# Late rows of an attention and feed-forward kernel: stores and loads moved to GpSimd's queue, differences to GpSimd, splits spread over steps, the order of the late part written out by hand

## The chip, the cores and the metric

One Trainium2 chip, one core. The metric is device time in microseconds (us) of one execution. Engines: PE (TensorE, matmuls), DVE (VectorE), ACT (ScalarE), POOL (GpSimd) and SP (SyncE, which here only issues transfers, "DMAs").

## The reference, cut to what matters

```
scores = q k^T / 8  + bias(distance, head);  only the last 96 keys and the first 8 are kept
a      = softmax(scores);   attn = a v          # 4 batches, 8 heads, 768 rows, 64 per head
x      = attn as 3072 rows of 512
out    = leaky_relu(x @ w_in, 0.01) @ w_out     # 512 -> 2048 -> 512, float32
```

## The kernel before

**Precision.** PE multiplies in a short float32 form, so every operand is kept as a high and a low part: `h = cast(x)` on ACT, then `l = x - h` on DVE ("a split"). Each product is three matmuls: high by high, low by high, high by low. Weights are `wih`, `wil` (first layer) and `woh`, `wol` (second).

**Feed-forward.** The 3072 rows are 24 attention steps of 128 rows. The first 18 are six plain chunks of three (384 rows, chunks 0 to 5). A chunk takes 16 *steps*; step `j` of 96 makes a block of 128 hidden values for a chunk (`hidden`, 12 matmuls L1031 to L1033 into `ps_h`), then PE does the output of the block before (`project`, 9 matmuls L1052 to L1054 into `ps_o`). Between the two stands a chain on other engines: ACT copies `ps_h` to `t` (L1035), DVE applies the leaky relu (L1036), ACT casts `gh` (L1041), DVE subtracts `gl` (L1042). `ps_h` is one buffer, so the next hidden block waits for the copy `t`; the output matmuls wait for `gh` and `gl`.

**The last six attention steps** (768 rows) go by Strassen's scheme, in eight *rounds* after step 95. A round has seven products of six matmuls (L611, into two banks `ps_p`), and in between 12 output groups of three matmuls for the round before (the first round has only three, those of step 95). Its inputs are the rows `b11`, `b12`, `b21`, `b22`, four differences of them (`t1` to `t4`, tile `diff`, L520), and sums of weight blocks `s1` to `s4`, which POOL makes ten additions a round (L541). Everything is split: rows at L516 (ACT) and L517 (DVE), sums at L547 and L548. In a round DVE also adds products (`u2`, `u3`, `t`, L629) and makes the four hidden blocks (`halves`, L622 to L624); ACT copies `u1` (L678) from the first product's bank before the third product may go on in it.

**Attention inside the steps.** In the late part attention is done in *visits* (two units each) put ahead of certain steps, `VISITS`. A visit's results for attention steps 15 to 23 can't stay on the chip: ACT copies them to `xo` (L355) and a DMA stores them to a buffer `xd` in memory (L356). Rows of chunk 5 are loaded back by `reload(j - RELOAD)` as one DMA into `xl` (L555) and split in four quarters, one in each of the next four steps (L558, L559). The rows of the Strassen part come back in `prepare(n)`, n = j - 96, at n = -4 (L512), and are split there and after.

**What sets the order.** Instructions under `pin` keep the program's order on their engine; the others are placed by a scheduler. PE's are all pinned. `pinned[0]` is set for each step: true up to step 22, for steps with a visit and while parts of a visit are left over; in the last steps and the Strassen part it is false, so there the scheduler chose. Waits are in order: an engine that waits for one instruction's input does nothing else. All DMAs of the main path but one are issued by SP.

Of the kernel before, what the change touches and what calls it, by code (L numbers as in the profile page):

```python
# [10 lines left out]
F32 = mybir.dt.float32  # L11
F32R = mybir.dt.float32r
# [6 lines left out]
P = 128  # L19
# [3 lines left out]
PAIRS = 22  # L23
HT = 384
SUPER = 2 * HT // P
VISITS = [39, 42, 46, 50, 54, 57, 61, 65, 68, 72, 76, 79, 83, 87, 90]
RELOAD = 70
TB = 32
G = 32
WIN = 96  # L30
# [21 lines left out]
def fast_path(ctx, tc, qp, kp, vp, wi, wo, nvec, weights, nmall, out, B, H, S):  # L52
# [45 lines left out]
    def pin(ins):  # L98

        if pinned[0]:  # L100
            tc.keep_in_program_order(ins)
# [248 lines left out]
    def high_x(u, av):  # L350
        if where(u)[0] >= SPILL:
            s, uu, i = where(u)
            units.pop(u)
            xo = att.tile([P, 2, P], F32, tag="work", name="xo", bufs=2)
            pin(nc.scalar.copy(out=xo, in_=av[:, :, 2 * KW:]))  # L355
            pin(nc.sync.dma_start(out=xd[:, 2 * uu:2 * uu + 2, (s - SPILL) * P:(s - SPILL + 1) * P], in_=xo))  # L356
            return
        pin(nc.scalar.copy(out=parts(u, 0), in_=av[:, :, 2 * KW:]))

# [145 lines left out]
        return n.rearrange("p (k t) -> p k t", k=2)  # L505

    def value(k):
        return late[k] if k in ("diff",) else late[k][1].bitcast(F32)

    def load_x(k):  # L510
        rows, cols = slice(2 * (k[1] == "2"), 2 * (k[1] == "2") + 2), slice(HT * int(k[2]), HT * int(k[2]) + HT)
        pin(nc.sync.dma_start(out=value(k), in_=xd[:, rows, cols]))  # L512

    def split_x(k, v=None):
        v = value(k) if v is None else v
        pin(nc.scalar.copy(out=late[k][0], in_=v))  # L516
        pin(nc.vector.tensor_tensor(out=late[k][1], in0=v, in1=late[k][0].bitcast(F32), op=ALU.subtract))  # L517

    def diff(in0, in1):
        pin(nc.vector.tensor_tensor(out=late["diff"], in0=value(in0), in1=value(in1), op=ALU.subtract))  # L520

    def block(n, f, m):
        return [weights[x][:, 2 * m:2 * m + 2, f * P:(f + 1) * P] for x in range(2)]
# [20 lines left out]
    def split_sum(i, k):  # L544
        if i >= NF // 2:
            return
        pin(nc.scalar.copy(out=late[k][0], in_=here[k]))  # L547
        pin(nc.vector.tensor_tensor(out=late[k][1], in0=here[k], in1=late[k][0].bitcast(F32), op=ALU.subtract))  # L548

    def reload(n):  # L550

        c = NCHUNK - 1
        if n == 0:
            xt[c] = [xts.tile([P, NK, CT], F32R, tag="xt", name=name) for name in ("xh", "xl")]
            pin(nc.sync.dma_start(out=xt[c][1].bitcast(F32), in_=xd[:, :, :CT]))  # L555
        elif 0 < n <= NK:
            hi, lo = (x[:, n - 1] for x in xt[c])
            pin(nc.scalar.copy(out=hi, in_=lo.bitcast(F32)))  # L558
            pin(nc.vector.tensor_tensor(out=lo, in0=lo.bitcast(F32), in1=hi.bitcast(F32), op=ALU.subtract))  # L559

# [2 lines left out]

    def prepare(n):

        if n == -4:
            early.close()
            pools["mem"] = mem = phase.enter_context(tc.tile_pool(name="late", bufs=1, side="right", reuse_waits="tile"))
            pools["ps"] = phase.enter_context(tc.tile_pool(name="ps_q", bufs=1, space=bass.MemoryType.PSUM, side="right", reuse_waits="tile"))
            pinned[0] = True  # L570
            for k in ("b11", "b21"):
                t = xts.tile([P, 4, HT], F32R, tag="xt", name=k)
                late[k] = [t[:, :2], t[:, 2:]]
            for k in ("b22", "t1", "t2", "t3", "t4"):
                late[k] = [mem.tile([P, 2, HT], F32R, name=k + x) for x in "hl"]
            late["b12"] = late["t3"]
            late["diff"] = mem.tile([P, 2, HT], F32, name="diff")
            for k in ("s1", "s2", "s3", "s4"):
                late[k] = [mem.tile([P, 2, P], F32R, name=k + x) for x in "hl"]
                here[k] = mem.tile([P, 2, P], F32, name=k)  # L580
            for k in ("b11", "b12", "b22", "b21"):
                load_x(k)
            make_sums(0)
        elif n == -3:
            diff("b12", "b11")
            split_x("t1", late["diff"])
            split_x("b11")
        elif n == -2:
            diff("b22", "diff")
            split_x("t2", late["diff"])  # L590
            diff("diff", "b21")
            split_sum(0, "s2")
            split_sum(0, "s3")
        elif n == -1:
            split_x("t4", late["diff"])
            diff("b22", "b12")
            split_x("t3", late["diff"])
            split_sum(0, "s1")

    def strassen():  # L600

# [23 lines left out]
            return gh, gl  # L625

        def add(name, in0, ps, op=ALU.add):
            t = mem.tile([P, HT], F32, name=name) if name else ffn.tile([P, HT], F32, name="t")
            pin(nc.vector.tensor_tensor(out=t, in0=in0, in1=ps, op=op))  # L629
            return t  # L630

# [26 lines left out]
        for i in range(NF // 2 + 1):  # L658
            if i:
                todo = [lambda n=n, g=g: second(g, n) for n in range(12)]  # L660
            else:
                todo = [lambda: ffn2(len(order) - 1, [n]) for n in range(3)]
                todo = [(lambda n=n: ffn2(len(order) - 1, [n])) for n in range(3)]

            def behind_(n):
                for _ in range(n):
                    if todo:
                        todo.pop(0)()
            if i == NF // 2:
                behind_(12)  # L670
                break
            b = blocks_of(i)
            x, y = banks[::-1] if i % 2 else banks
            gs = {}
            ps = x()
            product(b["a11"], "b11", ps)
            u1 = mem.tile([P, HT], F32, name="u1")
            pin(nc.scalar.copy(out=u1, in_=ps))  # L678
            split_sum(i, "s4")
            make_sums(i + 1)  # L680
            behind_(2 if i else 0)
            ps2 = y()
            product(late["s2"], "t2", ps2)
            u2 = add("u2", u1, ps2)
            split_sum(i + 1, "s2")
            if i == 0:
                split_x("b21")
            behind_(2 if i else 1)
            product(b["a12"], "b21", ps, first=False)
            t = ffn.tile([P, HT], F32, name="t")  # L690
            pin(nc.scalar.copy(out=t, in_=ps))
            gs[0, 0] = halves(t)
            behind_(2 if i else 1)
            product(late["s3"], "t3", ps2, first=False)
            u3 = add("u3", u1, ps2)
            split_sum(i + 1, "s3")
            if i == 0:
                split_x("b22")
            behind_(2 if i else 1)
            ps = x()  # L700
            product(late["s1"], "t1", ps)
            gs[1, 1] = halves(add(None, u3, ps))
            split_sum(i + 1, "s1")
            behind_(2)
            ps2 = y()
            product(b["a22"], "t4", ps2)
            gs[1, 0] = halves(add(None, u3, ps2, ALU.subtract))
            behind_(1)
            product(late["s4"], "b22", ps, first=False)
            gs[0, 1] = halves(add(None, u2, ps))  # L710
            behind_(12)
            g = i, gs
            if i == NF // 2 - 2:
                band_holds(tc, fl, nvec, nmall)
            if i == NF // 2 - 1:
                band_holds_everywhere(tc, fl, x()[0:1, 0:1], flag)
        phase.close()
        return flags[0]

# [23 lines left out]
    ps_o = ctx.enter_context(tc.tile_pool(name="ps_o", bufs=3, space=bass.MemoryType.PSUM))  # L743
    behind = []
    for j in range(len(order)):
        pinned[0] = j < half + NF or bool(behind) or any(t >= PAIRS for t in ev_at.get(j, ()))
        conv = list(conv_at.get(j, ()))
        for t in ev_at.get(j, ()):
            if t >= PAIRS:
                visit(t, behind)  # L750
            else:
                event(t, conv[:1])
            conv = conv[1:]

        def end():
            for step in due:
                step()
            due.clear()
            if behind:
                behind.pop(0)()  # L760

        def more():
            if behind:
                behind.pop(0)()
            for n, p in enumerate(conv):
                if n:
                    end()
                for step in conversion(p):
                    step()
        if j == half:  # L770

            scale_bias(tc, tabs[:, 1], nbw, H, 2)
            scale_bias(tc, tabs[:, 0, HALF:], nb0, H, 2)
        ffn1(j, end, more)
        if j:
            ffn2(j - 1)
        reload(j - RELOAD)
        prepare(j - len(order))
# [352 lines left out]
```

## Time and profile before

| what | value |
|---|---|
| three runs | 661.36, 663.00, 663.35 us; median 663.0 |
| the profiled execution | 661.57 us, of which the span of the profile is 660.0 |
| mean granted clock of PE | 0.986 |
| busy share | PE 95%, DVE 65%, ACT 44%, POOL 14% |

Times inside the profile count from the span's start. A step without a visit takes 4.2 us. Steps 70 and 71 lie at 372 to 395 us, the last visit (step 90) at 490, the first Strassen round at 524, the last output at 655. A line of the timeline gives start, duration, engine, line, operation, what is written and read, and in brackets how long the engine was idle before and what released it. "SPq" is the queue of DMAs that SP issues.

### The profile page before, as it was taken

To read this page: it belongs to the slowest core of one execution; us is meant where nothing else is said; L and a number is where in the kernel's file an instruction comes from. 1 tells how busy PE (TensorE), PEld (TensorE's weight loads), DVE (VectorE), ACT (ScalarE), POOL (GpSimd) and SP (SyncE) were. 2 spreads that over 40 slices of the span, in tenths; PEclk is the share of its full clock that TensorE was granted. 3 is DMA by queue.
4 is the path that set the end of the run, shared out by engine and by line. 5 is a ranking of instruction groups with operands and counts; after the bars stand their busy time and mean duration, and the time that the engine had idled before them with its cause. 6 is when DMAs were issued, how large, how long until landed. Compare 5 with 4: busy or idle time off the path is not lost. (4 is left out here: it accounts for less than half of the span.)

```text
span 660.0 us, 14710 instructions
## 1 busy us (share of the span) xinstructions
PE 629.0 (95%) x5692; PEld 550.8 (83%) x5692; DVE 429.1 (65%) x1191; ACT 293.0 (44%) x822; POOL 95.4 (14%) x128
## 2 busy tenths in 40 slices
PE   6699999999999999999999969999998899999996
PEld 4578898898888888988888858888886789888884
DVE  6888998886665475665755545565528676666642
ACT  6887755455443353444444424444325332222211
POOL 3213300000000000000000000000018255555300
PEclk9799999999999999999999979999999999999999
DMA  8876744414666345375656555557412010000002
GB/s 278 308 288 211 224 148 132 155 33 169 209 205 206 109 127 165 113 242 171 213 166 210 177 160 176 192 167 251 144 29 92 1 49 0 1 1 0 1 1 100
DMA packets 61677, 92.79 MB, mean 141 GB/s; under 512 B 10144, under 2 KB 36768, under 8 KB 61600
## 3 DMA queue, kind: packets, MB, share of 16 engines
q1 hardware_dynamic: 61456, 91.51, 42.9%
q8 instruction: 47, 0.77, 0.5%
q14 instruction: 30, 0.25, 0.1%
q10 hardware_dynamic: 144, 0.26, 0.1%
HBM read 70.26 MB, written 21.50 MB: 139 GB/s over the span
## 5 line engine op out<-in xcount | busy, mean ns | idle before, releaser
L1031 PE MATMUL ps_h<-xh,wih 128*128 128x384 f32 x384 | 133.7, 348 | 6.8 <-ACT t L1035 6.7
L1054 PE MATMUL ps_o<-woh,gl 128*128 128x512 f32 x336 | 133.9, 399 | 3.9 <-DVE gl L1042 3.7
L1052 PE MATMUL ps_o<-woh,gh 128*128 128x512 f32 x336 | 133.1, 396 | 0.6 <-ACT gh L1041 0.4
L1053 PE MATMUL ps_o<-wol,gh 128*128 128x512 f32 x336 | 132.6, 395 | 0.0
L1033 PE MATMUL ps_h<-xh,wil 128*128 128x384 f32 x384 | 130.2, 339 | 0.0
L1032 PE MATMUL ps_h<-xl,wih 128*128 128x384 f32 x384 | 130.1, 339 | 0.0
L1036 DVE SCALAR_TENSOR_TENSOR t<-t 128x384 f32<-128x384 f32 x96 | 57.7, 602 | 65.4 <-ACT t L1035 63.8
L1035 ACT COPY t<-ps_h 128x384 f32<-128x384 f32 x96 | 45.8, 477 | 122.1 <-PE ps_h L1033 121.9
L1031 PEld LDWEIGHTS ps_h<-xh,wih 128*128 128x128 f32 x384 | 72.6, 189 | 16.6 <-ACT t L1035 7.6
L222 ACT ACTIVATE pr<-pr,nmall 128x192 f32<-128x192 f32 (+1 forms) x192 | 83.6, 440 | 4.9 <-DVE nmall L207 4.9
L1054 PEld LDWEIGHTS ps_o<-woh,gl 128*128 128x128 f32 x336 | 63.2, 188 | 21.0 <-DVE gl L1042 6.5
L541 POOL TENSOR_TENSOR s<-wih 128x256 f32<-128x256 f32 x16 | 14.7, 922 | 455.4 <-PE ps_v L338 411.0
L1042 DVE TENSOR_TENSOR gl<-t,gh 128x384 fp32r<-128x384 f32 x96 | 54.4, 566 | 32.9 <-ACT gh L1041 32.9
L1032 PEld LDWEIGHTS ps_h<-xl,wih 128*128 128x128 f32 x384 | 72.7, 189 | 2.9
L1052 PEld LDWEIGHTS ps_o<-woh,gh 128*128 128x128 f32 x336 | 63.4, 189 | 11.5 <-ACT gh L1041 2.1
L1033 PEld LDWEIGHTS ps_h<-xh,wil 128*128 128x128 f32 x384 | 72.6, 189 | 0.1
L1053 PEld LDWEIGHTS ps_o<-wol,gh 128*128 128x128 f32 x336 | 63.2, 188 | 10.0
L1041 ACT CAST gh<-t 128x384 fp32r<-128x384 f32 x96 | 49.1, 511 | 44.6 <-DVE t L1036 43.9
L541 POOL TENSOR_TENSOR s<-s,wil 128x256 f32<-128x256 f32 x48 | 44.9, 940 | 3.0
L207 DVE CUSTOM_DVE_ANT_0 pr<-ps_v,nbw 128x192 f32<-128x192 f32 x88 | 25.3, 354 | 25.8 <-ACT xo L355 14.1
L623 ACT CAST gh<-t 128x384 fp32r<-128x384 f32 x32 | 16.4, 513 | 47.3 <-DVE t L622 45.6
L222 ACT ACTIVATION_READ_ACCUMULATOR pr<-pr,nmall 128x1 f32 x192 | 36.7, 191 | 0.0
(176 smaller groups left out, 926.0 us busy)
## 6 DMA issues: line engine op xcount, KB each, us to landing
kr<-in_kp_dram SPq DMA_DIRECT2D x40, 384.0 KB, 4.5
vr<-in_vp_dram SPq DMA_DIRECT2D x40, 320.0 KB, 5.1
via<-pr SPq DMA_DIRECT2D x30, 384.0 KB, 2.6
pt<-via SPq DMA_DIRECT2D x120, 96.0 KB, 2.4
wst<-in_wi_dram SPq DMA_DIRECT2D x16, 512.0 KB, 3.8
wst<-in_wo_dram SPq DMA_DIRECT2D x16, 512.0 KB, 4.1
qs<-in_qp_dram SPq DMA_DIRECT2D x24, 256.0 KB, 4.2
out_dram<-part SPq DMA_DIRECT2D x20, 256.0 KB, 2.9
```

The source lines that it names most:

```text
L222: pin(nc.scalar.activation(out=p, in_=p, func=AF.Exp, scale=-1.0, bias=nm[:, 2 * a + j:2 * a + j + 1], accum_out=sm[:, 2 * a + j:2 * a + j ...
L541: pin(nc.gpsimd.tensor_tensor(out=here[k], in0=acc_, in1=t, op=op))
L1031: tc.keep_in_program_order(nc.tensor.matmul(ps, lhsT=wih[:, k, fs], rhs=xh[:, k, :CT], start=(k == 0), stop=False))
L1032: tc.keep_in_program_order(nc.tensor.matmul(ps, lhsT=wih[:, k, fs], rhs=xl[:, k, :CT], start=False, stop=False))
L1033: tc.keep_in_program_order(nc.tensor.matmul(ps, lhsT=wil[:, k, fs], rhs=xh[:, k, :CT], start=False, stop=(k == NK - 1)))
L1035: pin(copy(out=t, in_=ps))
L1036: pin(nc.vector.scalar_tensor_tensor(out=t, in0=t, scalar=0.01, in1=t, op0=ALU.mult, op1=ALU.max))
L1041: pin(copy(out=gh, in_=t))
L1042: pin(nc.vector.tensor_tensor(out=gl, in0=t, in1=gh.bitcast(F32), op=ALU.subtract))
L1052: tc.keep_in_program_order(nc.tensor.matmul(o, lhsT=gh[:, ts_], rhs=woh[:, f, :], start=first, stop=False))
L1053: tc.keep_in_program_order(nc.tensor.matmul(o, lhsT=gh[:, ts_], rhs=wol[:, f, :], start=False, stop=False))
L1054: tc.keep_in_program_order(nc.tensor.matmul(o, lhsT=gl[:, ts_], rhs=woh[:, f, :], start=False, stop=last))
```

## The change

- Stores of `xo` and the loads of `xl` and of the `b` rows are issued by POOL instead of SP.
- `VISITS` moves up by up to two steps (last visit at 88, before 90); `RELOAD` is 68 instead of 70, and the four quarter splits of `xl` begin four steps after the load instead of one.
- The Strassen part's preparation is stretched from four steps to twelve: `b11`, `b21` are loaded at n = -12, `b12`, `b22` and the first sums at n = -8, one or two splits a step from n = -6. The four differences move from DVE to POOL and get two buffers.
- The check of the band (`band_holds`) moves from the last rounds to steps 88 and 89.
- From step 39 on everything goes in program order. In the rounds the code is put in another order: the additions that free a bank come before the leaky relu of the block ahead.

```diff
-VISITS = [39, 42, 46, 50, 54, 57, 61, 65, 68, 72, 76, 79, 83, 87, 90]
-RELOAD = 70
+VISITS = [39, 42, 46, 49, 53, 56, 60, 63, 67, 70, 74, 77, 81, 84, 88]
+RELOAD = 68
...
-            pin(nc.sync.dma_start(out=xd[:, 2 * uu:2 * uu + 2, (s - SPILL) * P:(s - SPILL + 1) * P], in_=xo))
+            pin(nc.gpsimd.dma_start(out=xd[:, 2 * uu:2 * uu + 2, (s - SPILL) * P:(s - SPILL + 1) * P], in_=xo))
...
-        pin(nc.sync.dma_start(out=value(k), in_=xd[:, rows, cols]))
+        pin(nc.gpsimd.dma_start(out=value(k), in_=xd[:, rows, cols]))
...
-    def diff(in0, in1):
-        pin(nc.vector.tensor_tensor(out=late["diff"], in0=value(in0), in1=value(in1), op=ALU.subtract))
+    def diff(name, in0, in1):
+        t = pools["mem"].tile([P, 2, HT], F32, tag="diff", name="diff", bufs=2)
+        pin(nc.gpsimd.tensor_tensor(out=t, in0=value(in0), in1=value(in1), op=ALU.subtract))
+        late[name] = t
...
-            pin(nc.sync.dma_start(out=xt[c][1].bitcast(F32), in_=xd[:, :, :CT]))
-        elif 0 < n <= NK:
-            hi, lo = (x[:, n - 1] for x in xt[c])
+            pin(nc.gpsimd.dma_start(out=xt[c][1].bitcast(F32), in_=xd[:, :, :CT]))
+        elif 4 <= n < 4 + NK:
+            hi, lo = (x[:, n - 4] for x in xt[c])
...
+        if n == -12:
+            for k in ("b11", "b21"):
...
+                load_x(k)
+        elif n == -8:
...
+            for k in ("b12", "b22"):
+                load_x(k)
...
             make_sums(0)
...
+            diff("d1", "b12", "b11")
+            band_holds(tc, fl, nvec, nmall)
+        elif n == -7:
+            band_holds_everywhere(tc, fl, pools["ps"].tile([P, HT], F32, tag="ps_p", name="ps_f")[0:1, 0:1], flag)
+        elif n == -6:
             split_sum(0, "s2")
             split_sum(0, "s3")
+        elif n == -5:
+            split_sum(0, "s1")
+            split_x("b11")
+        elif n == -4:
+            diff("d2", "b22", "d1")
+            split_x("t1", late["d1"])
+        elif n == -3:
+            split_x("t2", late["d2"])
+            diff("d4", "d2", "b21")
+        elif n == -2:
+            split_x("t4", late["d4"])
+            diff("d3", "b22", "b12")
+            split_x("b21")
         elif n == -1:
+            split_x("t3", late["d3"])
...
-            gs[1, 1] = halves(add(None, u3, ps))
+            c22 = add("t", u3, ps)
...
-            gs[1, 0] = halves(add(None, u3, ps2, ALU.subtract))
+            c21 = add(None, u3, ps2, ALU.subtract)
+            gs[1, 1] = halves(c22)
             behind_(1)
             product(late["s4"], "b22", ps, first=False)
-            gs[0, 1] = halves(add(None, u2, ps))
+            c12 = add(None, u2, ps)
+            gs[1, 0] = halves(c21)
+            gs[0, 1] = halves(c12)
...
-        pinned[0] = j < half + NF or bool(behind) or any(t >= PAIRS for t in ev_at.get(j, ()))
+        pinned[0] = j < half + NF or j >= VISITS[0]
```

Three places show how the order on an engine moves. First ACT around the reload, before: `xh` is the cast of a quarter of the reloaded rows, `t` and `gh` belong to a step's chain, `pr` to a visit.

```order
L222 ACTIVATE pr,sm<-pr,nmall 128x2x96 x2
L558 CAST xh<-xl 128x384 x2
L1035 COPY t<-ps_h 128x384
L1041 CAST gh<-t 128x384
L1035 COPY t<-ps_h 128x384
```

The same engine after:

```order
L1041 CAST gh<-t 128x384
L560 CAST xh<-xl 128x384
L1041 COPY t<-ps_h 128x384
L1047 CAST gh<-t 128x384
L560 CAST xh<-xl 128x384
L355 COPY xo<-ps_v 128x256 x2
```

Before, two casts of reloaded rows stand together, right ahead of a step's copy `t`; now there is one in each of four later steps, behind that step's `gh`.

Second ACT in steps 91 to 93, before (`b_6298` is `b11`, `b_6299` is `b21`, `diff` the difference that is split into `t1`, `t2`):

```order
L1035 COPY t<-ps_h 128x384
L516 CAST b_6298<-b_6298 128x768
L1041 CAST gh<-t 128x384
L547 CAST s1h<-s_6313 128x256
L516 CAST t1h<-diff 128x768
L516 CAST b22h<-b22l 128x768
L547 CAST s2h<-s_6316 128x256
L1035 COPY t<-ps_h 128x384
L516 CAST b_6299<-b_6299 128x768
L1041 CAST gh<-t 128x384
```

And after, from step 90 (`b_6009` is `b11`):

```order
L1041 COPY t<-ps_h 128x384
L1047 CAST gh<-t 128x384
L549 CAST s2h<-s_6203 128x256
L549 CAST s3h<-s_6206 128x256
L1041 COPY t<-ps_h 128x384
L1047 CAST gh<-t 128x384
L549 CAST s1h<-s_6200 128x256
L516 CAST b_6009<-b_6009 128x768
L1041 COPY t<-ps_h 128x384
L1047 CAST gh<-t 128x384
L516 CAST t1h<-diff 128x768
```

Before, casts of the preparation stand between a step's `t` and its `gh`; now each step's pair is together and the preparation's casts come behind it.

Third DVE in a late round, before, with buffer numbers (`u_6893` is `u3`, `u_6858` is `u2`):

```order
L629 TENSOR_TENSOR t<-u_6893,ps_p 128x384
L622 SCALAR_TENSOR_TENSOR t<-t 128x384
L629 TENSOR_TENSOR t<-u_6858,ps_p 128x384
L624 TENSOR_TENSOR gl<-t,gh 128x384
L622 SCALAR_TENSOR_TENSOR t<-t 128x384
L548 TENSOR_TENSOR s4l<-s_6322,s4h 128x256
```

And after (numbered: `t_6918` is the sum for the second block, `u3_6901` and `u2_6866` the third and fourth, now in place):

```order
L638 TENSOR_TENSOR u3_6901<-u3_6901,ps_p_6928 128x384
L631 SCALAR_TENSOR_TENSOR t_6918<-t_6918 128x384
L633 TENSOR_TENSOR gl_6937<-t_6918,gh_6936 128x384
L638 TENSOR_TENSOR u2_6866<-u2_6866,ps_p_6911 128x384
L631 SCALAR_TENSOR_TENSOR u3_6901<-u3_6901 128x384
L633 TENSOR_TENSOR gl_6461<-u3_6901,gh_6460 128x384
L631 SCALAR_TENSOR_TENSOR u2_6866<-u2_6866 128x384
```

The addition of the third block now stands ahead of the second block's leaky relu and `gl`, which stand ahead of the fourth's addition; so two low parts, each waiting for a cast on ACT, come before the fourth block's leaky relu.

More of the change, by code (lines that the diff above doesn't have):

```diff
@@ L507, in value @@
     def value(k):
-        return late[k] if k in ("diff",) else late[k][1].bitcast(F32)
+        return late[k] if k[0] == "d" else late[k][1].bitcast(F32)
     def load_x(k):
         rows, cols = slice(2 * (k[1] == "2"), 2 * (k[1] == "2") + 2), slice(HT * int(k[2]), HT * int(k[2]) + HT)
-        pin(nc.sync.dma_start(out=value(k), in_=xd[:, rows, cols]))
+        pin(nc.gpsimd.dma_start(out=value(k), in_=xd[:, rows, cols]))
     def split_x(k, v=None):
@@ L564, in prepare @@
     def prepare(n):
-        if n == -4:
+        if n == -12:
+            for k in ("b11", "b21"):
+                t = xts.tile([P, 4, HT], F32R, tag="xt", name=k)
+                late[k] = [t[:, :2], t[:, 2:]]
+                load_x(k)
+        elif n == -8:
             early.close()
@@ L569, in prepare @@
             pools["ps"] = phase.enter_context(tc.tile_pool(name="ps_q", bufs=1, space=bass.MemoryType.PSUM, side="right", reuse_waits="tile"))
[L570 to L573, printed above, removed]
             for k in ("b22", "t1", "t2", "t3", "t4"):
@@ L576, in prepare @@
             late["b12"] = late["t3"]
-            late["diff"] = mem.tile([P, 2, HT], F32, name="diff")
+            for k in ("b12", "b22"):
+                load_x(k)
             for k in ("s1", "s2", "s3", "s4"):
@@ L580, in prepare @@
                 here[k] = mem.tile([P, 2, P], F32, name=k)
-            for k in ("b11", "b12", "b22", "b21"):
-                load_x(k)
             make_sums(0)
[L584 to L591, printed above, removed]
+            diff("d1", "b12", "b11")
[3 more added lines that the diff above has]
+        elif n == -6:
             split_sum(0, "s2")
             split_sum(0, "s3")
+        elif n == -5:
[11 more added lines that the diff above has]
+            split_x("b21")
         elif n == -1:
[L595 to L598, printed above, removed]
+            split_x("t3", late["d3"])
     def strassen():
@@ L627, in add @@
         def add(name, in0, ps, op=ALU.add):
-            t = mem.tile([P, HT], F32, name=name) if name else ffn.tile([P, HT], F32, name="t")
+            t = in0 if name is None else ffn.tile([P, HT], F32, name="t") if name == "t" else mem.tile([P, HT], F32, name=name)
             pin(nc.vector.tensor_tensor(out=t, in0=in0, in1=ps, op=op))
@@ L685, in strassen @@
             split_sum(i + 1, "s2")
-            if i == 0:
-                split_x("b21")
             behind_(2 if i else 1)
@@ L706, in strassen @@
             product(b["a22"], "t4", ps2)
-            gs[1, 0] = halves(add(None, u3, ps2, ALU.subtract))
+            c21 = add(None, u3, ps2, ALU.subtract)
+            gs[1, 1] = halves(c22)
             behind_(1)
             product(late["s4"], "b22", ps, first=False)
-            gs[0, 1] = halves(add(None, u2, ps))
+            c12 = add(None, u2, ps)
+            gs[1, 0] = halves(c21)
+            gs[0, 1] = halves(c12)
             behind_(12)
             g = i, gs
[L713 to L716, printed above, removed]
         phase.close()
```

## The prediction

> **What bounds the kernel now.** I read the page's busy shares and slices first, then what PE waited for, then the timeline around each late gap.
>
> ```profile
> span 660.0 us, 14710 instructions
> PE 629.0 (95%) x5692; PEld 550.8 (83%) x5692; DVE 429.1 (65%) x1191; ACT 293.0 (44%) x822; POOL 95.4 (14%) x128
> ...
> PE   6699999999999999999999969999998899999996
> PEclk9799999999999999999999979999999999999999
> ```
>
> PE is the bound: it idles 660.0 - 629.0 = 31 us, at the start, in the 24th slice (379 to 396 us), in the 31st and 32nd (495 to 528) and at the end. The start is not touched by the change. The 24th slice also has a lower granted clock. What PE waited for in these places:
>
> ```profile
> PE ps_h L1031 <- ACT t L1035: 6.7, 2, 5.9
> PE ps_o L1054 <- DVE gl L1042: 3.7, 3, 2.0
> PE ps_p L611 <- DVE t L629: 0.6, 2, 0.3
> ```
>
> So there is one wait of 5.9 us for ACT's copy of a hidden block, and several of up to 2.0 us for DVE. In the visits between steps 39 and 70 PE waits for nothing. The long wait in the timeline, with the granted clock behind it from the table by stretches (its last five columns are POOL, clock, DMA share, GB/s):
>
> ```profile
> 379.46 0.40 PE L1054 MATMUL ps_o<-woh,gl 128*128 128x512 f32 x1
> ...
> 382.51 0.40 PE L1052 MATMUL ps_o<-woh,gh 128*128 128x512 f32 x1
> ...
> 383.08 0.54 SPq L555 DMA_DIRECT2D xl<-xd  x1
> ...
> 383.67 0.40 PE L1054 MATMUL ps_o<-woh,gl 128*128 128x512 f32 x1
> ...
> 388.66 0.92 ACT L558 CAST xh<-xl 128x384 fp32r<-128x384 f32 x2 [8.15 <-DMA xl<-xd]
> ...
> 389.49 0.47 ACT L1035 COPY t<-ps_h 128x384 f32<-128x384 f32 x1
> 390.02 0.69 PE L1031 MATMUL ps_h<-xh,wih 128*128 128x384 f32 x1 [5.95 <-ACT t L1035]
> ...
> 395.31 0.42 PE L1052 MATMUL ps_o<-woh,gh 128*128 128x512 f32 x1
> ```
>
> ```profile
> 390.02:395.31 5.29, 5.29 (x16) 5.00 (x17) 2.98 (x11) 0.99 (x2) 0.00 (x0) 0.50 0.28 74
> ```
>
> The load of chunk 5's rows is issued at 383.08 and landed by 388.66. Two casts of those rows stand in ACT's queue ahead of the copy `t`, so ACT sits 8.15 us and PE behind it 5.95. After that PE runs at half clock (0.50) until 395.31. The same 16 issues, one output matmul, 12 hidden and three output, take 382.51 - 379.46 = 3.05 us a step earlier and 395.31 - 383.67 = 11.64 here. The stall costs **8.6 us**.
>
> The Trainium skill, TensorE: Matmul & The Clock Gate, What's actually happening, says that the array falls to half clock after about 3.4 us of idling and needs as long a busy time to come back. The trace agrees in kind: half clock after 5.95 us of idling, though it lasts 5.3 us here.
>
> **The change part by part.**
>
> *The reload.* Its load goes out two steps earlier, and the first cast comes four steps behind it instead of one; each cast stands behind a step's `gh`. A step's length, and PE's starts through the late part:
>
> ```profile
> 481.41 0.34 PE L1031 MATMUL ps_h<-xh,wih 128*128 128x384 f32 x1
> 485.63 0.34 PE L1031 MATMUL ps_h<-xh,wih 128*128 128x384 f32 x1
> 495.87 0.34 PE L1031 MATMUL ps_h<-xh,wih 128*128 128x384 f32 x1
> ...
> 512.80 0.50 PE L1054 MATMUL ps_o<-woh,gl 128*128 128x512 f32 x1 [2.00 <-DVE gl L1042]
> 523.88 0.52 PE L611 MATMUL ps_p<-b,wih 128*128 128x384 f32 x2
> 533.87 0.62 PE L611 MATMUL ps_p<-b,wih 128*128 128x384 f32 x2 [0.34 <-DVE t L629]
> ...
> 581.84 0.52 PE L611 MATMUL ps_p<-b,wih 128*128 128x384 f32 x2
> ```
>
> A step is 485.63 - 481.41 = 4.22 us. Between the load at step 68 and the first cast in step 72 lie more than 4 x 4.22 = 17 us; the load took 5.6 us from issue to use. Even at twice that it is hidden, by 11 us of cover. The cast (0.46 us) and the subtraction beside it fit in a step in which ACT needs `t` and `gh`, about 1 us, of 4.22. I take the whole 8.6 us as gained; if a software-issued load needed over 17 us, the stall would return one for one.
>
> *The way into the Strassen part.* From 495.87 (step 91) to 523.88 (first round) PE takes 28.0 us for five steps that need 5 x 4.22 = 21.1: 6.9 lost. The 3.05 us above are 12 hidden and four output issues and 4.22 are 12 and nine, so an output matmul is 0.234 and a hidden one 0.176; a product is 1.06 us and an output group 0.70. The first round, seven products and three groups, needs 9.5 us and took 533.87 - 523.88 = 10.0: 0.5 lost. Rounds 1 to 3 took 581.84 - 533.87 = 47.97; a quiet round is 584.25 - 568.47 = 15.78 by the rows below: 0.6 lost. Together **8.0 us**. DVE is the reason:
>
> ```profile
> 488.47 0.56 DVE L1036 SCALAR_TENSOR_TENSOR t<-t 128x384 f32<-128x384 f32 x1 [2.48 <-ACT t L1035]
> ...
> 497.82 0.96 DVE L520 TENSOR_TENSOR diff<-t3l,b 128x768 f32<-128x768 f32 x1 [2.45 <-DMA t3l<-xd]
> ...
> 508.38 1.09 DVE L1036 SCALAR_TENSOR_TENSOR t<-t 128x384 f32<-128x384 f32 x1
> 509.39 1.49 DVE L520 TENSOR_TENSOR diff<-diff,b 128x768 f32<-128x768 f32 x1
> ```
>
> ```profile
> 491.77 0.74 POOL L541 TENSOR_TENSOR s<-wih 128x256 f32<-128x256 f32 x1 [410.97 <-PE ps_v L338]
> ...
> 501.02 3.33 POOL L541 TENSOR_TENSOR s<-s,wil 128x256 f32<-128x256 f32 x3
> ```
>
> While POOL adds, each DVE operation with two inputs in SBUF takes 0.53 us more (1.09 for 0.56, 1.49 for 0.96), and POOL's own go from 0.74 to 1.11 (3.33 / 3). The scheduler put most of these ahead of a step's chain. The change takes four differences off DVE (4 x 0.96 to 1.49 us), lets the splits begin in step 90 instead of 92, and puts each behind a chain that is done. A chain is `t`, relu, `gh`, `gl`, about 2.1 us quiet and 3.2 beside POOL, for a step of 4.22, so steps 90 to 95 should run nearly clean; for the four differences on POOL I take 0.6 us in all (from 0 to 2, one quarter to one half of an operation held up each time). For POOL, 768 columns are unseen; between 0.74 and 3 x 1.11 us, I take 2.2 = 3 x 0.74, since the length is three times. They are due a step or more later.
>
> What stays is the first round: `t3` is split there, `b22` and `s4` too, with nothing but three groups between the products. Before product 7 (due 6 x 1.06 + 3 x 0.70 = 8.5 us into the round) DVE has two operations of 768 columns and nine smaller ones: 2 x 0.96 + 9 x 0.56 = 7.0 us, starting 0.1 to 1.2 late behind `gl`; beside POOL up to 7 x 0.53 = 3.7 more. So 7.1 to 11.9 us against 8.5: PE waits 0 to 3.4, I take 1.7, the middle. The lateness goes on into round 1, 0 to 1.4, I take 0.7. Residue 0.6 + 1.7 + 0.7 = **3.0 us** (0 to 6.8), so 5.0 are gained.
>
> The Trainium skill, SBUF — State Buffer, Who interferes with whom, says that DVE with two SBUF inputs and a GpSimd operation that reads SBUF lock each other out for whole instructions. The row's 0.53 is less than a whole 0.74. By that rule a DVE operation caught by a difference would wait up to an estimated 2.2 us, the chain would come to 4.3, and four of them would cost up to 3 us more: the sum would be 651.
>
> *POOL's queue of transfers.* What SP shows for the same transfers, in the timeline and in the list of DMAs (last number: median us from issue to landing):
>
> ```profile
> 491.27 1.74 SPq L356 DMA_DIRECT2D xd<-xo  x2
> ...
> 493.97 0.36 SPq L512 DMA_DIRECT2D t3l<-xd  x1
> ```
>
> ```profile
> t3l<-xd SPq DMA_DIRECT2D x1, 384.0 KB, 3.7
> b22l<-xd SPq DMA_DIRECT2D x1, 384.0 KB, 5.7
> ```
>
> The load of `b12` could be issued 2.7 us after the first store. On POOL the sums of round 0 stand behind stores and loads. Count from the start of step 88's hidden block: sums could begin at about 3.5 us on SP's times; POOL's issue is unseen, I take 2 us more in all (0 to 8). The cast of `s3` in step 90 needs the eighth sum, 8 x 0.74 to 8 x 1.11 = 5.9 to 8.9 us later, and must be done by 16.3, or step 91's `t` is late. Begin at 5.5, done by 14.4: nothing lost; the bound is 7.4 to 10.4. Stores in earlier visits have POOL to themselves. SP, freed of these, has fewer DMAs ahead of the visits' own: 0.
>
> *Rounds.* Same matmuls, DVE's order differs:
>
> ```profile
> 568.47 0.47 ACT L678 COPY u<-ps_p 128x384 f32<-128x384 f32 x1
> 570.96 0.52 PE L611 MATMUL ps_p<-b,wih 128*128 128x384 f32 x2
> ...
> 582.71 1.09 DVE L622 SCALAR_TENSOR_TENSOR t<-t 128x384 f32<-128x384 f32 x1
> 583.83 0.51 ACT L623 CAST gh<-t 128x384 fp32r<-128x384 f32 x1 [2.01 <-DVE t L622]
> 584.25 0.47 ACT L678 COPY u<-ps_p 128x384 f32<-128x384 f32 x1
> ```
>
> Now product 3 starts at 570.96, 2.0 us after the copy `u1` ended. After the change `u1` stands behind a chain from product 6: addition, relu, `gl`, addition, relu, `gl`, relu on DVE with three casts between, then the copy: 7 x 0.56 + 3 x 0.51 + 0.47 = 5.9 us. PE from product 6 to the next round's product 3: six groups and three products, 7.4. Five of those DVE operations have two SBUF inputs, 5 x 0.53 = 2.7 beside POOL. Slack between +1.5 and -1.2 us; with half of them beside POOL, +0.2: 0 lost, in seven rounds at most 8.
>
> *Rest.* The earlier visits, the band's check and the end: the same work; 0, with 0.5 either way.
>
> **Sum.** 661.6 - 8.6 - 5.0 = 648.0 against the profiled execution (span 660.0, 1.6 around it). The median of three runs is 1.4 above that execution; I take half and say **648.7**.
>
> **Rivals.** (a) Every round waits for `u1`: POOL keeps DVE busy through the chain, 0.5 to 1 us in seven rounds, 652 to 656. For it: 1.09 at 582.71 right in this chain. Against: POOL has only ten sums in 15.8 us. (b) The way in stays as slow, residue 6 to 7 instead of 3: 652. (c) The wait for the reload only moves to another transfer, the change not doing what it says: 657 to 663. Against: 17 us of cover. (d) Slower: POOL's stores and loads at step 88 take so long that `s3` holds up ACT, then `t`, then PE, one for one once the sums begin after 7.4 to 10.4 us. A gap that long also brings the half clock seen at 390 us, 2.5 of the 8.6 us. To eat 13.6 us the gap must be about 11, sums at about 20 us, where SP's times give 3.5; then 663 to 670.
>
> **How the numbers follow.** My forecast 0.65, (a) 0.14, (b) 0.13, (c) 0.03, (d) 0.04, rest 0.01. The forecast's own range, residue 0 to 6, is 645 to 651. The range for 8 in 10 takes in most of (a) and (b): 645.2 to 654.5. About 0.3% (2 us) can't be told from no change; faster is forecast, (a), (b) and half of (c): 0.94; same 0.02, slower 0.04.
>
> **What would show it.** Right: no wait of PE over 3 us after 100 us, clock 1.00 around step 71, ACT's cast of `xl` not waiting for a DMA, PE's waits from step 90 to round 1 together about 3 us and mostly at L620 (the products' new line), rounds of 15.8 us. Wrong: rounds over 16.1 us, or ACT waiting for POOL's sums at L549, or POOL's DMAs followed by long idling ahead of L543.

## The result, and the profile after

The changed kernel takes 646.1 us (median of 4 runs, 644.3 to 647.4) against 662.2 us of the kernel before on the same chip: ratio 0.975, 95% interval 0.972 to 0.979. Medians in this document are of the fast executions; two slow ones, 873 us of the changed kernel and 2087 us of a variant, are left out. The forecast was 648.7 us, range 645.2 to 654.5. The profiled execution after took 644.86 us, span 643.3, so 16.7 us less than the profiled execution before.

The page after, first its busy shares, then PE and its granted clock in 40 slices:

```profile
span 643.3 us, 14742 instructions
PE 621.2 (97%) x5692; PEld 546.9 (85%) x5692; DVE 424.6 (66%) x1187; ACT 291.4 (45%) x822; POOL 119.5 (19%) x155
...
PE   5699999999999999999999999999999999999996
PEclk9899999999999999999999999999999999999999
```

The dents of before in the 24th, 31st and 32nd slices are gone, and so is the slow clock in the 24th. What PE still waited for in the part that was changed (waited for, us in total, times, longest):

```profile
PE ps_p L620 <- DVE t L638: 0.9, 1, 0.9
...
PE ps_p L620 <- ACT u L687: 0.6, 1, 0.6
...
PE ps_p L620 <- DVE u L638: 0.2, 1, 0.2
```

All three lie in rounds 0 and 1, together 1.7 us. The steps before them run clean: five steps from step 91's hidden block to the first product take 506.49 - 485.51 = 20.98 us, where before they took 28.0.

```profile
485.51 0.34 PE L1037 MATMUL ps_h<-xh,wih 128*128 128x384 f32 x1
...
506.49 0.51 PE L620 MATMUL ps_p<-b,wih 128*128 128x384 f32 x2
```

At the reload, the load on POOL's queue and the first cast on ACT:

```profile
375.98 0.79 POOL L557 DMA_DIRECT2D xl<-xd  x1 [5.00 <-PE ps_h L1039]
...
397.58 0.51 ACT L1047 CAST gh<-t 128x384 fp32r<-128x384 f32 x1 [2.10 <-DVE t L1042]
398.00 0.51 ACT L560 CAST xh<-xl 128x384 fp32r<-128x384 f32 x1
```

The cast waits for no DMA. Not all of the 16.7 us comes from the change. The same matmul of step 39's visit, ahead of which the two programs are alike, stands here before and here after:

```profile
229.44 0.45 PE L326 MATMUL ps_v<-pt,vr 64*64 64x128 f32 x8
```

```profile
227.58 0.45 PE L326 MATMUL ps_v<-pt,vr 64*64 64x128 f32 x8
```

So 1.9 us of the difference is scatter of the start, and in these two executions the late part is 16.7 - 1.9 = **14.8 us** shorter, where the sum said 13.6.

### The profile page after: what moved, and what is told of

Same layout as the page of the kernel before. It is cut to its first block, busy times and chain, and to the rows that moved or that the text cites. A ratio compares the mean times of both kernels' runs of the same rounds, so it can differ in the third digit from the quotient of the medians.

```text
span 643.3 us, 14742 instructions
## 1 busy us (share of the span) xinstructions
PE 621.2 (97%) x5692; PEld 546.9 (85%) x5692; DVE 424.6 (66%) x1187; ACT 291.4 (45%) x822; POOL 119.5 (19%) x155
## 5 line engine op out<-in xcount | busy, mean ns | idle before, releaser
L1042 DVE SCALAR_TENSOR_TENSOR t<-t 128x384 f32<-128x384 f32 x96 | 59.3, 618 | 59.5 <-ACT t L1041 57.8
L356 POOL DMA_DIRECT2D xd<-xo x18 | 13.3, 740 | 374.1 <-ACT xo L355 374.0
L1047 ACT CAST gh<-t 128x384 fp32r<-128x384 f32 x96 | 49.1, 511 | 48.9 <-DVE t L1042 48.1
L543 POOL TENSOR_TENSOR s<-s,wil 128x256 f32<-128x256 f32 x48 | 43.6, 909 | 3.8
L249 DVE TENSOR_SCALAR pr<-pr,rs 128x192 f32<-128x192 f32 (+1 forms) x136 | 33.7, 312 | 1.0
```

Source lines behind the costliest of these rows:

```text
L543: pin(nc.gpsimd.tensor_tensor(out=here[k], in0=acc_, in1=t, op=op))
L1042: pin(nc.vector.scalar_tensor_tensor(out=t, in0=t, scalar=0.01, in1=t, op0=ALU.mult, op1=ALU.max))
L1047: pin(copy(out=gh, in_=t))
```

## The experiments

The start scatters by more than some of the effects sought, so the variants of the changed kernel are also compared by their late stretch: the span less the start of the first copy `xo`, up to which they scatter from 333.6 to 337.2 us. Up to there they are all one program but for the kernel that is not pinned, which differs from step 39 on. The late stretch comes from one profiled execution of each. Two of the rows it is read from (the shortest, least, median and longest duration in ns, then the first and the last start), of the changed kernel and of it with the differences on DVE:

```profile
L355 ACT COPY xo<-ps_v x18: 372/373/374, 333.7 to 472.7; 128x256 f32<-128x256 f32 x18
```

```profile
L355 ACT COPY xo<-ps_v x18: 372/372/374, 334.5 to 473.4; 128x256 f32<-128x256 f32 x18
```

| kernel | median, us | ratio to before, interval | late stretch, us |
|---|---|---|---|
| changed, again | 645.4 | 0.975 (0.973 to 0.977) | 309.4 (first profile 309.6) |
| casts 1 step behind the load | 646.7 | 0.977 (0.975 to 0.980) | 309.7 |
| steps 39 to 91 not pinned | 656.2 | 0.992 (0.990 to 0.994) | 318.1 |
| splits bunched | 655.5 | 0.992 (0.988 to 0.995) | 318.5 |
| differences on DVE | 644.1 | 0.974 (0.971 to 0.978) | 308.0 |
| transfers on SP | 647.9 | 0.980 (0.976 to 0.984) | 309.7 |
| POOL's sums 5.9 us later | 649.3 | 0.982 (0.980 to 0.984) | 311.8 |
| rounds in the old order | 647.1 | 0.978 (0.976 to 0.980) | 310.2 |
| differences on DVE, `s4` early | 645.6 | 0.975 (0.973 to 0.977) | 309.1 |
| *before*, casts 4 steps behind the load | 662.2 | 1.001 (0.999 to 1.003) | |
| *before*, pinned | 660.9 | 0.998 (0.996 to 1.000) | |
| *before*, pinned, `b21` early | 658.2 | 0.995 (0.993 to 0.997) | |

The variants of the kernel before have no late stretch to compare, since their visits stand at other steps. The runs were made in three sets on three chips, and each ratio is to the kernel before in the same set (medians 661.6, 661.7 and 661.8 us). The changed kernel's late stretch is taken as 309.5, the mean of its two.

**The kernel before with the casts four steps behind the load.**

```
-        elif 0 < n <= NK:
-            hi, lo = (x[:, n - 1] for x in xt[c])
+        elif 4 <= n < 4 + NK:
+            hi, lo = (x[:, n - 4] for x in xt[c])
```

> The kernel before, with one edit: the reload's four casts and subtractions stand four to seven steps behind its load instead of one to four; the load itself, the way into the Strassen part and everything else are as before. Theory A (my prediction's: the distance in steps between load and first cast removes the stall): the 8.6 us are gained, 653 to 654 us, and no wait of PE over 3 us near 385 us. Theory B (what counts is whether the casts are pinned behind a step's chain; these steps are not pinned, and in the program's order the first two casts still stand ahead of the copy t that PE waits for): the stall of 6 us and the slow clock behind it stay, 662 us as before.

662.2 us, ratio 1.001: nothing gained. ACT, and PE behind it:

```profile
386.47 0.92 ACT L558 CAST xh<-xl 128x384 fp32r<-128x384 f32 x2 [7.16 <-DMA xl<-xd]
387.30 0.47 ACT L1035 COPY t<-ps_h 128x384 f32<-128x384 f32 x1
```

```profile
387.82 0.69 PE L1031 MATMUL ps_h<-xh,wih 128*128 128x384 f32 x1 [4.95 <-ACT t L1035]
```

Two casts still stand right ahead of the copy `t`, four steps in the code or not. Theory B.

**The changed kernel with the casts one step behind the load** (the same four lines, the other way round, pinned as they are).

> The changed kernel, with one edit: the reload's casts stand one to four steps behind its load again, pinned. Theory A (distance in steps): 8.6 us lost again, 654 to 655 us. Theory B (pinned order): the first cast stands behind the next step's gh, about 5.7 us after the load's issue, and the load takes 6.0; ACT waits 0.4 us and has 1.9 us to spare before PE notices, so 646 us, no change within 1 us.

646.7 us: nothing lost. The first cast waits 0.59 us for the load, behind a finished chain, and PE does not wait:

```profile
382.74 0.51 ACT L1047 CAST gh<-t 128x384 fp32r<-128x384 f32 x1 [0.63 <-DVE t L1042]
383.84 0.51 ACT L560 CAST xh<-xl 128x384 fp32r<-128x384 f32 x1 [0.59 <-DMA xl<-xd]
```

**The changed kernel, steps 39 to 91 not pinned outside visits.**

```
-        pinned[0] = j < half + NF or j >= VISITS[0]
+        pinned[0] = j < half + NF or bool(behind) or any(t >= PAIRS for t in ev_at.get(j, ())) or j >= len(order) - 4
```

> The changed kernel, with one edit: steps 39 to 91 are pinned only in visits, as before the change; the last four steps and the rounds stay pinned. The reload's cast is still four steps behind its load in the code, but in the program's order the first two casts now stand ahead of an earlier step's copy t. Theory A (distance in the code): 646 us as the changed kernel. Theory B (pinned order): the stall is back, 7 to 9 us, 653 to 655 us, with ACT idle about 6 to 8 us for the load and half clock behind it.

656.2 us, the late stretch 318.1 against 309.5: **8.6 us**. Counted from step 39's visit, up to which the two are one program, it is the same: 424.3 us to the end against 415.7. The stall is back, with the half clock (third number from the end, in the table by stretches) behind it:

```profile
383.54 0.92 ACT L560 CAST xh<-xl 128x384 fp32r<-128x384 f32 x2 [7.20 <-DMA xl<-xd]
```

```profile
384.89 0.69 PE L1037 MATMUL ps_h<-xh,wih 128*128 128x384 f32 x1 [5.00 <-ACT t L1041]
```

```profile
384.89:390.20 5.31, 5.31 (x16) 5.02 (x17) 3.02 (x11) 0.99 (x2) 0.00 (x0) 0.50 0.30 74
```

The stall and the slow clock behind it (half of 5.31) are 5.00 + 2.65 = 7.65 of the 8.6 us; the rest is lost from step 91 on, where PE waits another 0.5 us for `gh`. So the agreement with the 8.6 us that the prediction read from the longer stall of before is in part chance.

The three runs show what removed the stall: not the two steps that the load goes out earlier and not the three that the cast comes later, but the order on ACT's queue, with a cast behind `gh`, where a late load costs little, and not ahead of `t`.

**The kernel before, pinned from step 39** (run `pin_alone`; its old line for `pinned[0]` replaced by the new one).

> The kernel before, with one edit: from step 39 on every instruction is pinned to the order of the program, as in the changed kernel; the casts still stand one to four steps behind the load. Theory A (distance in steps): the first cast is one step behind the load as before, so most of the 8.6 us stay lost, 660 to 662 us. Theory B (pinned order): the first cast stands behind the next step's gh, 4.2 + 1.1 us after the copy it stood ahead of before, when the load of 5.6 us has about landed; 8.3 to 8.6 us gained there. On the way into the Strassen part the wide operations now stand behind the chains, but up to five of them in one step (step 94: 4.6 us and a chain of 2.1 to 3.2 in 4.22), so the 8 us lost there stay within 2: 651 to 656 us.

660.9 us, 0.7 less than before in the same set (661.6) and not sure to be less at all. The number is in theory A's range, but not for its reason: the reload's part went nearly as theory B has it, PE waits 1.5 us there instead of 5.9, and another wait took the rest. What PE waited for, then the load and its first cast, then ACT and POOL in round 0:

```profile
PE ps_p L611 <- ACT b L516: 9.1, 1, 9.1
...
PE ps_h L1031 <- ACT t L1035: 1.5, 1, 1.5
```

```profile
390.90 0.54 SPq L555 DMA_DIRECT2D xl<-xd  x1
```

```profile
396.39 0.51 ACT L558 CAST xh<-xl 128x384 fp32r<-128x384 f32 x1 [4.66 <-DMA xl<-xd]
```

```profile
521.23 0.41 ACT L547 CAST s2h<-s 128x256 fp32r<-128x256 f32 x1 [4.49 <-POOL s L541]
521.54 0.83 ACT L516 CAST b<-b 128x768 fp32r<-128x768 f32 x1
```

```profile
517.16 0.84 POOL L541 TENSOR_TENSOR s<-wih 128x256 f32<-128x256 f32 x1 [24.27 <-DVE s1l L548]
```

POOL can't begin round 1's sums before DVE has split `s1` of round 0, which frees the buffer, and in this order `s1` is split at the end of step 95. ACT's cast of the new `s2` waits 4.49 us for those sums, the cast of `b21` stands behind it, and product 3 needs `b21`. Pinning removes most of the wait for the load and makes one for the sums. What stays of the first comes from the load, which goes out on SP's queue only in step 71, right behind a visit's transfers `pt`, 7.3 us after step 70's hidden block began (383.57); in the changed kernel with the casts one step behind, POOL issued it 2.2 us after step 68's (375.08), and PE did not wait.

**The same with `b21` split ahead of the next round's `s2`.**

```
-            split_sum(i + 1, "s2")
             if i == 0:
                 split_x("b21")
+            split_sum(i + 1, "s2")
```

> The kernel before with the order pinned from step 39 (the run pin_alone, 661.0 us, where PE waited 9.1 us in round 0 for ACT's cast of b21), with one more edit: in round 0 the split of b21 stands ahead of the split of the next round's sum s2 instead of behind it. Theory C (ACT's queue: the cast of b21 stood behind the cast of s2, which waited 4.49 us for POOL's sums of round 1): product 3 can start about when DVE is through with b21, near 518.9 instead of 522.4 on that trace; 3 to 5 us gained, 656 to 658 us, and what stays of the 9.1 us is DVE's work. Theory D (DVE has too much to do in the last steps, whatever stands on ACT): the wait stays, 660 to 661 us.

658.2 us, 2.7 less by the medians, in another set of runs and with intervals that overlap: theory C's mechanism, a little short of its 3 to 5 us. The wait falls from 9.1 to 4.2 us, and the waits for DVE in `ps_p` rise from 1.2 to 2.8 and take part of its place:

```profile
PE ps_p L611 <- ACT b L516: 4.2, 1, 4.2
PE ps_p L611 <- DVE t L629: 2.8, 2, 1.6
```

**The changed kernel with the splits bunched** (the added lines; the same splits are taken out of the places that "The change" shows).

```
         elif n == -3:
+            split_x("t1", late["d1"])
+            split_x("b11")
             diff("d4", "d2", "b21")
         elif n == -2:
+            split_x("t2", late["d2"])
             diff("d3", "b22", "b12")
+            split_sum(0, "s2")
+            split_sum(0, "s3")
         elif n == -1:
+            split_x("t4", late["d4"])
             split_x("t3", late["d3"])
+            split_sum(0, "s1")
...
+            if i == 0:
+                split_x("b21")
```

> The changed kernel with the splits bunched as before the change: t1 and b11 in step 93, t2, s2 and s3 in step 94, t4, t3 and s1 in step 95, b21 in round 0 behind the next round's s2; the differences stay on POOL, the transfers on POOL's queue and the order pinned. Theory C (the spread is what lets POOL begin round 1's sums early, since s1's split frees their buffer): the stall of pin_alone comes back, PE waits 6 to 9 us for ACT's cast of b21, 652 to 656 us. Theory D (only DVE's load per step counts): the four differences are off DVE, steps come to 4.0 to 5.5 us for 4.22, 1 to 4 us lost, 647 to 650 us.

655.5 us, the late stretch 9.0 us longer: theory C. POOL begins round 1's sums at 511.23 instead of 503.18, after a wait of 4.31 us for the split of `s1`. PE has no wait in the steps themselves, and in round 0 this one:

```profile
515.30 0.41 ACT L549 CAST s2h<-s 128x256 fp32r<-128x256 f32 x1 [4.15 <-POOL s L543]
515.61 0.83 ACT L516 CAST b<-b 128x768 fp32r<-128x768 f32 x1
```

```profile
516.49 0.69 PE L617 MATMUL ps_p<-b,wih 128*128 128x384 f32 x1 [7.06 <-ACT b L516]
```

So pinning needs the spread: pinned without it, round 0 loses what the reload gained. This edit moves both the split of `s1` and that of `b21`; which of the two weighs how much here, and whether the spread would do without pinning in the last four steps and the rounds, no run shows.

**The differences on DVE** (run `diff_dve`).

```
-        pin(nc.gpsimd.tensor_tensor(out=t, in0=value(in0), in1=value(in1), op=ALU.subtract))
+        pin(nc.vector.tensor_tensor(out=t, in0=value(in0), in1=value(in1), op=ALU.subtract))
```

> The changed kernel with the four differences on DVE instead of POOL. My prediction's view (they load DVE; 4 x 0.96 us come back, less what a step's slack hides): 0 to 2 us slower, 646 to 648 us, with DVE's operations in steps 91 to 95 no longer stretched to 1.5 to 2.2 us. Rival (POOL's differences are what makes the way in clean): 4 us or more slower, 650 us or more. Rival (the port shared by POOL and DVE costs more than it saves): 1 to 2 us faster, 644 to 645 us.

644.1 us; the late stretch is 1.5 us shorter than the changed kernel's, where 0 to 2 longer was my view and 1 to 2 shorter the second rival's. One wait is left in the rounds, and POOL's sums for round 1 begin at 491.30 instead of 503.18:

```profile
PE ps_p L620 <- ACT u L687: 0.6, 1, 0.6
```

```profile
491.30 0.74 POOL L543 TENSOR_TENSOR s<-wih 128x256 f32<-128x256 f32 x1 [3.45 <-DVE s1l L550]
```

In the changed kernel those sums stand in POOL's queue behind the last two differences, so POOL is at work beside DVE in round 0; here eight of the ten are done before it.

**All transfers back on SP** (`nc.gpsimd.dma_start` to `nc.sync.dma_start` in three places).

> The changed kernel with all stores and loads of the last blocks' rows issued by SP again, at the same places of the program. My prediction's view (the queue is worth nothing either way; POOL's sums begin 1 to 3 us earlier, which nobody waits for): 646 us, no change within 1 us. Rival (SP's queue is what was in the way, since a store that waits for ACT holds up the visits' loads of q, k and v behind it): PE waits appear in the visits from step 67 on, 2 us or more slower, 648 us or more.

647.9 us, ratio 0.980 against 0.975 with intervals that overlap, and the late stretch 309.7 against 309.5; PE's waits in the rounds are 1.9 us against 1.7, with none new in the visits. POOL's sums begin 0.2 us after the start of step 88's hidden block (473.93) instead of 4.8. With the casts four steps behind their load, the queue is worth nothing that shows. It does decide when the reload goes out:

```profile
387.66 0.54 SPq L557 DMA_DIRECT2D xl<-xd  x1
```

That is about 10 us later than from POOL (375.98, in an execution that runs 1.5 us ahead), because on SP the load stands behind a visit's transfers `pt`, which wait for an earlier one (`via`). It has landed 5 us ahead of the first cast (398.05). One step behind its load that cast would stand at about 383, ahead of this issue: the distance and the queue each cover for the other. The changed kernel with both taken away was not run.

**POOL's sums late.**

```
+            a = blocks_of(0)["a21"][0].bitcast(F32)
+            for n in range(8):
+                pin(nc.gpsimd.tensor_tensor(out=here["s1"], in0=a, in1=a, op=ALU.add))
             make_sums(0)
```

> The changed kernel with eight more additions of 128x256 on POOL ahead of round 0's sums (their results are overwritten by the sums), which is as if POOL's transfers had taken 6.2 to 6.6 us longer: the sums begin at about 11 us after the start of step 88's hidden block instead of 4.6. My prediction's bound (7.4 to 10.4 us) says that the cast of s3 then holds up ACT, the copy t of step 91 and PE. Worked out on the trace of the changed kernel: the cast of s3 ended at 485.91 and would end at 492.2, t 4.8 us late with 2.1 us of cover: 2 to 4 us slower than the changed kernel, 648 to 650 us, with a wait of PE for ACT's t of 2 to 4 us near step 92. Rival (there is more slack than that, since the load of the queue shifts everything behind it alike): 0, 646 us.

649.3 us, 3.9 more by the medians of this set; the late stretch 2.3 us longer. The extra work took 5.85 us, the cast of `s3` ended at 491.14, and PE waited twice, 2.0 us together:

```profile
491.58 0.45 PE L1040 MATMUL ps_h<-xh,wih 128*128 128x384 f32 x1 [1.48 <-ACT t L1044]
...
494.88 0.50 PE L1063 MATMUL ps_o<-woh,gl 128*128 128x512 f32 x1 [0.48 <-DVE gl L1051]
```

So the bound of the prediction is real: sums that begin 11.0 us after step 88's hidden block (483.69 against 472.73) cost 2.0 us. If a us of lateness costs a us, the cost sets in near 9 us, and the changed kernel, at 4.8, is some 4 us short of that.

**The rounds in the old order.**

```
-            c22 = add("t", u3, ps)
+            gs[1, 1] = halves(add("t", u3, ps))
...
-            c21 = add(None, u3, ps2, ALU.subtract)
-            gs[1, 1] = halves(c22)
+            gs[1, 0] = halves(add(None, u3, ps2, ALU.subtract))
...
-            c12 = add(None, u2, ps)
-            gs[1, 0] = halves(c21)
-            gs[0, 1] = halves(c12)
+            gs[0, 1] = halves(add(None, u2, ps))
```

> The changed kernel with the rounds' order of before: each of the last three blocks is halved right behind its addition (c22, c21, c12), not one product later. My prediction's view (PE has 7.4 us of its own work where the chain needs 5.9 in either order): 0, 646 us, no change within 1 us. Rival (the reordering is what keeps the rounds free of waits): 0.5 us a round or more, 650 us.

647.1 us, 1.7 more by the medians of this set with overlapping intervals; late stretch 0.7 us longer, waits 2.4 us instead of 1.7, all in round 0 and at the start of round 1; the later rounds are as clean as before:

```profile
PE ps_p L620 <- DVE u L638: 1.5, 2, 1.2
...
PE ps_p L620 <- DVE t L638: 0.9, 1, 0.9
```

The new order is worth about 0.7 us once, and not 0.5 us in each round.

**Differences on DVE and `s4` early**, beside the changed kernel again.

```
             split_sum(0, "s1")
+            split_sum(0, "s4")
...
-            split_sum(i, "s4")
+            if i:
+                split_sum(i, "s4")
```

> The changed kernel with the four differences on DVE (the run diff_dve, 644.1 us) and with the split of s4 for round 0 moved from round 0 into step 91. Theory: in diff_dve one wait of 0.6 us is left in the rounds (product 3 of round 1 for ACT's copy u1), and POOL's last two sums of round 1 stand 9.33 us behind that split of s4; with it early, POOL is done before round 0 and DVE has 0.42 us less there, so the wait goes to 0 to 0.3 us: 643.5 to 644 us, 1 to 3 us faster than the changed kernel. Rival (the gain of diff_dve was chance between runs): no difference from the changed kernel, 646 us.

> The changed kernel as it is, on the same chip as the three others of this set, to compare them with: 646 us, 0.975 to 0.977 of the kernel before.

645.6 against 645.4 us, ratios 0.9752 and 0.9754: no difference that can be told. The theory was wrong on its point: all of POOL's sums for round 1 are done before round 0, and the wait for `u1` is as long as it was:

```profile
526.20 0.61 PE L621 MATMUL ps_p<-b,wih 128*128 128x384 f32 x2 [0.57 <-ACT u L688]
```

What holds `u1` there was not tried. In this trace the copy stands on ACT behind the fourth block's cast, which waits for a leaky relu that takes 1.09 us beside a sum of POOL, where 0.56 is quiet:

```profile
524.13 1.09 DVE L632 SCALAR_TENSOR_TENSOR u<-u 128x384 f32<-128x384 f32 x1
```

That is the mechanism of the prediction's rival (a), and the extra 0.53 us is about the size of this wait, but no run shows that it is the cause. Neither version with the differences on DVE is shown to be faster than the changed kernel: one median is 2.0 us lower than the changed kernel's first, in another set of runs, the other 0.2 higher in its own set, and the late stretches are 1.5 and 0.4 us shorter.

## Why the prediction was right, and where not

*The reload, 8.6 us gained.* Right in size: from step 39's visit to step 91 PE takes 485.51 - 227.58 = 257.9 us where it took 495.87 - 229.44 = 266.4, so 8.5 came. The reason was one of three that the prediction gave in a row. "Between the load at step 68 and the first cast in step 72 lie more than 4 x 4.22 = 17 us" is true and was not what counted: with one step between them nothing was lost, and in the unpinned kernel before, four steps in the code gained nothing, since the first two casts still came out ahead of `t`. What counted was "each cast stands behind a step's `gh`". By order alone 1.5 us of waiting stayed (the kernel before, pinned); in the changed kernel either POOL's queue, which sends the load out sooner, or the distance is enough to cover that rest, and the prediction put the queue's part at nothing.

*The way in, 5.0 us gained of 8.0.* 5.7 came: from step 91 to round 4 PE took 581.84 - 495.87 = 85.97 us before and takes 565.74 - 485.51 = 80.23 after.

```profile
517.56 0.52 PE L620 MATMUL ps_p<-b,wih 128*128 128x384 f32 x2
...
565.74 0.52 PE L620 MATMUL ps_p<-b,wih 128*128 128x384 f32 x2
```

The term that was mis-sized is the residue, 2.3 us by the same starts and not 3.0. Four differences on POOL were given 0.6 us and cost PE nothing in the steps (20.98 us for a need of 21.1); round 0 was given 1.7 and lost 517.56 - 506.49 - 9.5 = 1.6; rounds 1 to 3 were given 0.7 and lost 48.18 - 47.34 = 0.8. The reason put first, that the change "takes four differences off DVE", was no gain that shows: on DVE the late stretch is 1.5 us shorter. It was the second and third clauses, the splits begun in step 90 and each behind a chain; the prediction did not see that without the spread a pinned ACT would wait for POOL's sums, which the runs pinned without it price at about 9 us.

*POOL's queue, 0 lost.* Right. The sums began 4.8 us after step 88's hidden block (472.54), not 5.5:

```profile
472.63 1.53 POOL L356 DMA_DIRECT2D xd<-xo  x2 [15.06 <-ACT xo L355]
475.71 0.74 POOL L512 DMA_DIRECT2D t3l<-xd  x1 [1.55 <-DMA xd<-xo]
...
477.37 0.75 POOL L543 TENSOR_TENSOR s<-wih 128x256 f32<-128x256 f32 x1
...
486.44 2.03 POOL L521 TENSOR_TENSOR diff<-t3l,b 128x768 f32<-128x768 f32 x1
488.55 1.91 POOL L521 TENSOR_TENSOR diff<-b22l,diff 128x768 f32<-128x768 f32 x1
```

The four differences take 1.85 to 2.14 us each, where 2.2 was estimated. Rival (d) would have needed sums far beyond the bound that the run with late sums met.

*The rounds, 0 lost.* Right: a round without waits takes 569.58 - 553.80 = 15.78 us, to the hundredth as before, and `u1` is waited for once, not in each round as rival (a) has it.

```profile
553.80 0.47 ACT L687 COPY u<-ps_p 128x384 f32<-128x384 f32 x1
569.58 0.47 ACT L687 COPY u<-ps_p 128x384 f32<-128x384 f32 x1
```

*The rest, 0 with 0.5 either way.* From round 4 to the end 0.6 us is gained, which no run explains. The profiled executions differ by 1.9 us ahead of the change, so the 0.5 was too narrow for one execution's start. The medians differ by 16.1 us where the forecast, from a median of 663.0, said 14.3.

*The lock between POOL and DVE.* The rule of the Trainium skill, SBUF — State Buffer, Who interferes with whom, that the two exclude each other for whole instructions, describes these rows better than the 0.53 us that the prediction read beside additions of 0.74 us:

```profile
486.68 2.07 DVE L550 TENSOR_TENSOR s3l<-s,s3h 128x256 fp32r<-128x256 f32 x1
488.68 2.20 DVE L1042 SCALAR_TENSOR_TENSOR t<-t 128x384 f32<-128x384 f32 x1
...
493.43 0.55 DVE L1042 SCALAR_TENSOR_TENSOR t<-t 128x384 f32<-128x384 f32 x1
```

They begin within 0.3 us of the first two differences on POOL and end within 0.5 us of them; the second takes 1.65 us more than the same operation quiet. Yet the 651 us that the prediction worked out by that rule did not come either: a chain of 2.1 us with 1.65 on top still fits into a step of 4.22.

## What to carry to other kernels

Look at what stands next in an in-order queue behind each wait, not at how far apart two instructions are in the code: a cast of late data cost 0 to 1.5 us behind the chain that the bound engine needs, and about 8 us ahead of it. Two safeguards can cover for each other, as the distance and the issuing queue do here: taking away one of them shows nothing. An order written out by hand is only as good as its next wait; pinning alone moved the stall from a load to a sum, and it paid in full only with the splits spread, which free the buffer that the sum needs some steps earlier. To price effects of a microsecond, compare stretches from a common instruction, since the start of this program alone scatters by more.

## What the runs showed of the hardware

Stalls of 4.95, 5.00, 5.95 and 7.06 us put PE at half clock (0.50) for 5.3 us afterwards, alike in four kernels, so about a third of the cost of the stall of before comes behind it (2.6 of 8.6 us); after one of 4.21 us (the kernel before, pinned, `b21` early) the mean over the next 5.3 us is 0.56. A wait of 2.00 us in the kernel before (at 512.80) and one of 1.5 in the kernel with late sums left the clock at full (1.00):

```profile
491.58:497.00 5.42, 4.93 (x24) 4.18 (x25) 4.84 (x5) 1.93 (x4) 4.86 (x3) 1.00 0.00 0
```

A transfer's issue keeps POOL for 0.74 to 0.79 us in the rows above, and its transfers land about as fast as those of SP: `xd` in 3.3 us (from SP 4.2 before and 5.4 in the changed kernel), `xl` in 6.0 (5.6 and 5.1).

```profile
xd<-xo POOLq DMA_DIRECT2D x18, 128.0 KB, 3.3
...
xl<-xd POOLq DMA_DIRECT2D x1, 768.0 KB, 6.0
```
